# First chunk's C product as seven block products, last features of a strip in one GELU, some skips and seventh products added by transfers

## The chip, the cores and the metric

The kernel runs on one core of a Trainium2 chip. A core has a matrix engine (TensorE, PE in the profile), a vector engine (VectorE, DVE), an activation engine (ScalarE, ACT), a general engine (GpSimd, POOL) and a queue engine (SyncE, SP), which run side by side, each through its own instructions in the order of the program, and wait for each other by semaphores. Sixteen DMA engines move data. The metric is the device time of one execution in microseconds (us); less is better.

## The reference

The input x has 2048 tokens of D = 640 features, all in bfloat16. A diagonal linear recurrence with 640 complex states and a two-layer GELU network run on the same x; a gate per token mixes them:

```python
g = _sigmoid((x * gate_w).sum(-1, keepdims=True))
# recurrence: h = Lam_bar * h + B_bar @ x_t, for every token t in order
a = 2.0 * einsum("blp,dp->bld", hseq, Cmat).real + x * Dskip
# network, F = 1728
b = gelu(x @ w1 + b1) @ w2 + b2
return g * a + (1 - g) * b
```

## The kernel before

The tokens are cut into 4 chunks of 512 (`CH`). Each chunk c goes through four stages, each of which keeps TensorE streaming:

- `ff1(c)`: x @ w1 for the chunk, 13 tiles of 5 matmuls of 128x512 (L307) and a last tile of 20 small ones (L331), with a GELU on ScalarE (L316) that writes `gel`. The last features of a strip are a tile of 128 rows of which 96 go to `gel` and 32 to a helper tile `eL`, in two activations, and `load_e` brings the 32 to their place by a transfer. The gate's number for each token comes out beside it (`gz`), from which `gates(c)` (L647) makes the columns of factors `gcol`, on GpSimd, on VectorE for the last chunk.
- `ssm(c)`: B @ x, 50 matmuls (L481), evicted by ScalarE into `bu` (L484), and then the recurrence on VectorE: the state is turned by cosines and sines (`cos_in`, `sin_in`, `sum_in`, L556), scanned by two scan instructions (L573) and turned back (`cos_out`, `sin_out`, `sum_out`), into `hs[c]`. Five such groups a chunk. Four small ScalarE operations (L592) turn the end of each scan into the start of the next chunk's (`carry`).
- `fin_b(c)`: the product with w2, as a 2x2 block product with seven instead of eight block products (98 matmuls of 128x320, L738). Sums of blocks of `gel` are needed for that: a negation on ScalarE (`minus`, L687) and accumulating transfers on GpSimd's queue (`plus`, L682), together in `minus_c` and `minus_d`; for chunk 0 in `first_sums` on VectorE. The results go into tiles `gb`, scaled by half of one minus the gate (L758). `fork` copies a bank of PSUM into another with ScalarE (L750), so that two outputs can share a product. Product 7 goes into `gq` and is added to both halves of the output by an accumulating transfer (`twice`).
- the product of the states with C, and the final mix. For chunks 1 to 3 `fin_s(c)` (L900) does it with seven block products of 10 matmuls of 128x320 (L914): 70 in all, 65 for chunk 3. Its sums of blocks of `hs[c]` are M7, M6, M3 and g21 (`sum_7`, `sum_6`, `h_sums`), those of C are U7 and U6 (`sums_76`, VectorE, L875) and U5 and U4. Product 7 is added to `gb` by VectorE (`part_7`, L941), and the skip x * Dskip, times the gate, by `skip_in` (L890). Where `GS` has a tile for it (chunks 2 and 3), the scaled skip of the chunk's second half is written by ScalarE (`gated`) and added whole. `done` (L929) scales a finished bank by the gate, adds `gb` and writes `ot`, which goes out by a transfer.
- For chunk 0 `fin_a` (L806) does it plainly: 80 matmuls (L819) of 128x320 on eight banks into which ScalarE has copied the skip before (`seed`, L670, L674), and eight evictions on VectorE (L824).

In TensorE's order the stages are: ff1(0) and ssm(0) woven, ff1(1), ssm(1), fin_b(0), ff1(2), fin_a(0), ssm(2), fin_b(1), fin_s(1), ssm(3), ff1(3), fin_b(2), fin_s(2), fin_b(3), fin_s(3).

The order of each engine's instructions is fixed by the program text and by a small planner in it. `ck.pe`, `ck.act` and `ck.dve` are the planner's clocks. An operation of VectorE goes into a list with a due time and a cost (`later`); `let_out` emits those that are due, and `dve_now` emits one at once after those due before it. `scan_ops` weaves the operations of one group of the recurrence into those of the group before it. `let_out(0, c)`, the first line of `sum_7`, emits all of chunk c's recurrence that is still in the list. The rest is written by hand: a dictionary such as `{2: lambda: sum_7(1)}` calls steps in a stage's hook of that number (in `ff1` before a tile, in `ssm` before a group, in `fin_b` and `fin_s` after a product). The last lines (L1010 to L1062) are this plan.

PSUM has eight banks that are handed out in turn (`bank`); a matmul that starts a bank waits until its last reader is done. GpSimd's transfers run through one queue in order, SyncE's and ScalarE's through others.

Of the kernel before, what the change touches and what calls it, by code (L numbers as in the profile page):

```python
# [32 lines left out]
FA = 6  # L33
# [9 lines left out]
def kernel(  # L43
# [69 lines left out]
    eL = const.tile([P, CH], BF16, name="eL")  # L113
# [197 lines left out]
    def ff1_act(p, c, kf):  # L311
        s = kf if kf < FA else kf + 1 if kf < 2 * FA else FA
        for p0, p1 in ((0, RE), (RE, P)) if s == FA else ((0, P),):
            dst = eL[p0:p1, :] if p0 else gel[c][p0:p1, :, s, :]
            src = p[p0:p1, :] if p0 else p[p0:p1, :].rearrange("p (i t) -> p i t", i=2)
            nc.scalar.activation(out=dst, in_=src, func=ACT.Gelu_apprx_tanh, bias=b1_c[p0:p1, kf:kf + 1])  # L316
            act(0.69)
# [26 lines left out]
    def load_e(c):  # L344
        nc.sync.dma_start(out=gel[c][F_LAST:RE, :, KF - 1, :], in_=eL[RE:P, :].rearrange("p (i t) -> p i t", i=2))
# [17 lines left out]
    def gel_tile(c):  # L363
        gel[c] = gelp.tile([P, 2, KF, HT], BF16, name="gel")
        nc.gpsimd.memset(gel[c][RE:P, :, KH - 1, :], 1.0)
# [42 lines left out]
    part(1, 1)  # L408
    part(0, 3)
# [4 lines left out]
    turn_first(2, pA, pT)  # L414
# [232 lines left out]
    def gates(c):  # L647
# [3 lines left out]
        def f():  # L651
            for i, (m, b) in enumerate(((0.5, 0.5), (-0.5, 0.5), (0.5, -0.5), (-0.5, -0.5))[:4 if c > 0 else 3]):
# [8 lines left out]
    HALVES = ((0, HD), (HD, D))  # L661
    seeded = {}

    def cuts(ti):
        return ((0, HD), (HD, 512), (512, D)) if ti == NT - 1 else HALVES

    def skip(ti):
        dve_now(ck.pe, 0.4, lambda: nc.vector.tensor_tensor(out=xn[ti][:], in0=xn[ti][:], in1=Dbc[:], op=ALU.mult))

    def seed(ti):  # L670
        seeded[ti] = []
        for d0, d1 in cuts(ti):
            p = bank()
            nc.scalar.activation(out=p[:, 0:d1 - d0], in_=xn[ti][:, d0:d1], func=ACT.Identity)  # L674
            act(0.45)
            seeded[ti].append(p)
        if ti % TPC < TPC - 2:
            skip(ti + 2)
        if ti + TPC < NT - H:
            load_xn(ti + TPC)  # L680
# [43 lines left out]
    def twice(dst, src):  # L724
        plus(dst.rearrange("p (h d) -> p h d", h=2), src[:].rearrange("p (o d) -> p o d", o=1).to_broadcast([P, 2, HD]))

    def fin_b(c, at={}, gs=None):
# [54 lines left out]
        if c == NCH - 1:  # L782
            part_7()
            for j in range(H):
                twice(gs[j], gq[j])
# [5 lines left out]
        if c == NCH - 2:  # L791
            for j in range(H):
                twice(gs[j], gq[j])
# [5 lines left out]
        for j in range(0 if gs else H):  # L799
            twice(gbs[c * TPC + H + j][:], gq[j])  # L800
# [4 lines left out]

    def fin_a(c, at={}):  # L806
        let_out(0, c)
        for a in range(TPC):
            ti = c * TPC + a
            ot = fwork.tile([P, D], BF16, name="ot", bufs=4)  # L810
            if a < TPC - 2:
                seed(ti + 2)
            if a in at:
                at[a]()
            for i, (d0, d1) in enumerate(cuts(ti)):
                p = seeded[ti][i]
                for j in range(2 * KS):
                    CT = CT_re if j < KS else CT_im
                    nc.tensor.matmul(p[:, 0:d1 - d0], lhsT=hs[c][:, a // H, j // KS, j % KS, (a % H) * P:][:, 0:P], rhs=CT[:, j % KS, d0:d1],  # L819
                                     start=False, stop=(j == 2 * KS - 1), skip_group_check=True)  # L820
                    pe(d1 - d0)

                def f():
                    nc.vector.scalar_tensor_tensor(out=ot[:, d0:d1], in0=p[:, 0:d1 - d0], scalar=gcol[:, 0, ti:ti + 1],  # L824
                                                   in1=gbs[ti][:, d0:d1], op0=ALU.mult, op1=ALU.add)

                dve_now(ck.pe + 0.2, 0.45, f)
# [265 lines left out]
```

## Time and profile before

| what | us |
|---|---|
| median of three runs | 205.31 (205.02 to 208.02) |
| the profiled run | 205.97 |
| its span in the profile | 204.2 |
| TensorE busy | 199.4 |
| VectorE busy | 187.9 |
| ScalarE busy | 141.9 |
| GpSimd busy | 77.7 |

The span reaches from the first to the last instruction of the profile; 1.77 us of the run's time lie outside it. Of the chain that ended last, the page gives these shares by line:

```profile
PE 95%; DMA 2%; DVE 1%; SPq 0%; issue 0%; DVEq 0%
PE bank L307 27%; PE bank L738 26%; PE bank L481 21%; PE bank L914 14%; PE bank L819 5%; DMA xn<-in_A_x_dram 2%; PE bank L331 1%; DVE ot L929 0%; SPq L143 0%; PE bank L269 0%; DVEq L1088 0%; DVE colA L411 0%; PE bank L410 0%; PE bank L421 0%
```

A pair such as "PE bank L738" is an engine, the tile it wrote and the line. In a timeline a row is: start, length, engine, line, operation, output<-inputs, shape, count, and in brackets how long the engine had been idle before it and what it had waited for. A length includes the part in which the next instruction has already begun; where costs are summed, the distance of starts is meant.

### The profile page before, as it was taken

The numbers are of one execution on the slowest core, as the hardware profiler recorded it, in microseconds if no ns is written. First come the engines' busy times: TensorE is split into PE (matmuls) and PEld (weight loads), VectorE is DVE, ScalarE is ACT, GpSimd is POOL, SyncE is SP. The second block draws the span as 40 slices with busy tenths as digits, with TensorE's granted clock in tenths as the row PEclk, the third lists the DMA queues.
The fourth block names the chain that finished last, engine by engine and source line by source line (L and its number), as shares of the span: only waits on it lengthen the run. The fifth ranks groups of instructions, "written<-read, shape, count | busy, mean of one in ns | idle before, by whom it ended". The sixth has DMA issues, their size and how long they took to land.

```text
span 204.2 us, 3625 instructions
## 1 busy us (share of the span) xinstructions
PE 199.4 (98%) x1291; PEld 118.7 (58%) x1291; DVE 187.9 (92%) x292; ACT 141.9 (70%) x273; POOL 77.7 (38%) x119
## 2 busy tenths in 40 slices
PE   8899999999999999999999999999999999999994
PEld 5744544444467644676446777544446777777763
DVE  2589999999999999999999999999999999999574
ACT  3498766987867898993667674297786899245620
POOL 8385399952331299032031360032150370114000
PEclk9999999999999999999999999999999999999999
DMA  7999999999699092229878998149997699819403
GB/s 185 201 142 240 201 276 164 206 231 278 113 137 239 13 166 75 64 52 205 237 131 186 235 191 130 64 104 221 289 230 148 113 204 195 176 36 207 64 0 128
DMA packets 46374, 33.06 MB, mean 162 GB/s; under 512 B 27026, under 2 KB 42804, under 8 KB 46356
## 3 DMA queue, kind: packets, MB, share of 16 engines
q0 software_dynamic: 7040, 15.05, 42.4%
q1 hardware_dynamic: 38740, 17.29, 35.4%
q10 hardware_dynamic: 576, 0.49, 0.8%
q8 instruction: 10, 0.16, 0.3%
q14 instruction: 8, 0.07, 0.1%
HBM read 7.79 MB, written 2.62 MB: 51 GB/s over the span
## 4 chain that ended last, share of the span: by engine, by line
PE 95%; DMA 2%; DVE 1%; SPq 0%; issue 0%; DVEq 0%
PE bank L307 27%; PE bank L738 26%; PE bank L481 21%; PE bank L914 14%; PE bank L819 5%; DMA xn<-in_A_x_dram 2%; PE bank L331 1%; DVE ot L929 0%; SPq L143 0%; PE bank L269 0%; DVEq L1088 0%; DVE colA L411 0%; PE bank L410 0%; PE bank L421 0%
## 5 line engine op out<-in xcount | busy, mean ns | idle before, releaser
L316 ACT ACTIVATE gel<-bank,colB 128x512 bf16<-128x512 f32 (+1 forms) x52 | 33.6, 688 | 8.2 <-PE bank L307 7.9
L573 DVE TENSOR_TENSOR_SCAN g<-r_c,carry,v 128x512 bf16<-128x512 f32 x30 | 38.5, 1284 | 0.0
L738 PEld LDWEIGHTS <-gel 128*128 128x128 bf16 x280 | 27.3, 98 | 11.1 <-issue 0.2
L484 ACT ACTIVATE bu<-bank 128x512 bf16<-128x512 f32 x40 | 22.8, 601 | 15.4 <-PE bank L481 15.3
L738 PE MATMUL bank<-w_sb,gel 128*128 128x320 bf16 x168 | 24.3, 299 | 0.0
L758 ACT ACTIVATE gb<-bank,gcol 128x320 f32<-128x320 f32 x32 | 16.1, 527 | 7.9 <-PE bank L738 7.9
L307 PEld LDWEIGHTS <-w1a_sb 128*128 128x128 bf16 x162 | 14.0, 99 | 12.0
L307 PE MATMUL bank<-xB,w1a_sb 128*128 128x512 bf16 x90 | 19.9, 380 | 0.0
L481 PE MATMUL bank<-xB,BT_re 128*128 128x512 bf16 x75 | 18.6, 380 | 0.0
L481 PE MATMUL bank<-xB,BT_im 128*128 128x512 bf16 x75 | 18.6, 379 | 0.0
L481 PEld LDWEIGHTS <-BT_im 128*128 128x128 bf16 x100 | 9.8, 98 | 11.8
L481 PEld LDWEIGHTS <-BT_re 128*128 128x128 bf16 x100 | 9.6, 98 | 11.0
L914 PEld LDWEIGHTS <-hs 128*128 128x128 bf16 x125 | 12.0, 98 | 4.5
L929 DVE SCALAR_TENSOR_TENSOR ot<-bank,gcol,gb 128x320 bf16<-128x320 f32 (+2 forms) x25 | 12.5, 535 | 1.9 <-PE bank L914 1.2
L556 DVE TENSOR_TENSOR v<-wa,bu 128x1024 bf16<-128x1024 bf16 x20 | 13.8, 688 | 0.1
L556 DVE TENSOR_TENSOR wb<-TCOS,g 128x1024 bf16<-128x1024 bf16 x20 | 13.8, 689 | 0.0
L556 DVE TENSOR_TENSOR hs<-wb,bu 128x1024 bf16<-128x1024 bf16 x20 | 13.7, 687 | 0.0
L556 DVE TENSOR_TENSOR bu<-TSIN,g 128x1024 bf16<-128x1024 bf16 x20 | 13.8, 688 | 0.0
L556 DVE TENSOR_TENSOR wa<-TCOS,bu 128x1024 bf16<-128x1024 bf16 x20 | 13.4, 672 | 0.3 <-ACT bu L484 0.3
L556 DVE TENSOR_TENSOR bu<-TSIN,bu 128x1024 bf16<-128x1024 bf16 x20 | 13.5, 676 | 0.1
L307 PE MATMUL bank<-xB,w1b_sb 128*128 128x512 bf16 x60 | 13.4, 380 | 0.0
L738 PEld LDWEIGHTS <-N 128*128 128x128 bf16 x112 | 11.0, 98 | 4.3
(201 smaller groups left out, 401.6 us busy)
## 6 DMA issues: line engine op xcount, KB each, us to landing
out_dram<-ot SPq DMA_DIRECT2D x15, 160.0 KB, 2.4
w_sb<-in_B_w_dram SPq DMA_DIRECT2D x4, 480.0 KB, 5.8
gel<-N POOLq DMA_DIRECT2D x4, 448.0 KB, 4.9
N<-gel POOLq DMA_DIRECT2D x3, 448.0 KB, 5.1
gel<-gel POOLq DMA_DIRECT2D x3, 448.0 KB, 7.6
N<-N POOLq DMA_DIRECT2D x3, 448.0 KB, 7.5
gb<-gq POOLq DMA_DIRECT2D x4, 320.0 KB, 6.7
xn<-in_A_x_dram SPq DMA_DIRECT2D x8, 160.0 KB, 5.9
```

Of the source, the lines that this page charges most:

```text
L307: nc.tensor.matmul(p[:, t0:t1], lhsT=w, rhs=xT[c][:, kd, t0:t1], start=(kd == 0) if first is None else first, stop=(kd == last), skip_grou ...
L316: nc.scalar.activation(out=dst, in_=src, func=ACT.Gelu_apprx_tanh, bias=b1_c[p0:p1, kf:kf + 1])
L331: nc.tensor.matmul(p[:, a * NL:(a + 1) * NL], lhsT=xT[c][:, kd, a * P:(a + 1) * P], rhs=w1c[kd][:, n1c - NL:n1c], start=False, stop=(kd == ...
L481: nc.tensor.matmul(p[:], lhsT=BT[ks >= KSA][:, kd, (ks % KSA if ks < KSA else ks - KSA) * P:][:, 0:P], rhs=xT[c][:, kd, :], start=(kd == 0 ...
L484: nc.scalar.activation(out=bu[:, ri, :], in_=p[:], func=ACT.Identity)
L556: nc.vector.tensor_tensor(out=o, in0=a, in1=b, op=op)
L573: nc.vector.tensor_tensor_scan(s["g"][:, ri, :], r_c[:, ks:ks + 1].to_broadcast([P, CH]), s["v"][:, ri, :], init, ALU.mult, ALU.add)
L738: nc.tensor.matmul(p[:, 0:HD], lhsT=lhs[:, s, j * P:(j + 1) * P], rhs=rhs[:, s, :], start=fresh and s == 0, stop=s == KH - 1, skip_group_c ...
L758: nc.scalar.activation(out=gbs[ti][:, h * HD:(h + 1) * HD], in_=quad[j][name][:, 0:HD], func=ACT.Identity, scale=gcol[:, 1, ti:ti + 1])
L819: nc.tensor.matmul(p[:, 0:d1 - d0], lhsT=hs[c][:, a // H, j // KS, j % KS, (a % H) * P:][:, 0:P], rhs=CT[:, j % KS, d0:d1], start=False, s ...
L914: nc.tensor.matmul(t[j][:, d0:d1], lhsT=A[i][:, k, j * P:(j + 1) * P], rhs=B[i][:, k, d0:d1], start=fresh and k == 0, stop=k == KS - 1, sk ...
L929: dve_now(ck.pe + 0.2, 0.47, lambda: nc.vector.scalar_tensor_tensor(out=ots[ti][:, o + d0:o + d1], in0=t[j][:, d0:d1], scalar=gcol[:, 0, t ...
```

## The change

Chunk 0's C product goes through `fin_s(0)`; `fin_a`, `seed`, `cuts`, `seeds` and `sums` are removed. For that, M7 of chunk 0 is formed by a negation in the last hook of `fin_b(0)` and `sum_7(0, False)` behind it; `sums_76` moves from behind `fin_a(0)` to behind `fin_b(0)`; U5 is made by VectorE, U4 by a copy (SyncE) and an accumulation; `sum_6(0)` stands in `ff1(2)`; M3 takes M7's place in `fin_s(0)`'s hook 1. `skip_in` adds the skip for all four tiles on VectorE. Product 7 of chunks 0 and 2 is scaled by ScalarE and added by two transfers (`by_dma`) instead of by `part_7`.

The 128 rows of a strip's last features are written by one GELU into `gel`, from where `load_e` takes the 32; `ones_row(c)` then overwrites them with ones, which `gel_tile` did before at the start. It has its own place in the plan for each chunk. `gates(0)` moves to `ff1(1)` and makes four columns instead of three, `gates(1)` to `ff1(2)`, `gates(2)` from before `ssm(2)` to behind it. `first_sums` moves from tile 9 to tile 12 of `ff1(1)`.

`minus_c(1)` and `minus_d(1)` move from `fin_a(0)` into `ssm(2)`, `sum_7(1)` there from group 2 to group 3. For chunks 2 and 3 `skip_by_dma` scales half of a skip on ScalarE and adds it by a transfer, in the place of one half of `skip_in`. `minus_c(3)` moves one hook down. In the head, `turn_first(2)` stands before the `prmA` matmul.

```diff
--- before.py
+++ after.py
...
@@ -310,11 +309,9 @@
 
     def ff1_act(p, c, kf):
         s = kf if kf < FA else kf + 1 if kf < 2 * FA else FA
-        for p0, p1 in ((0, RE), (RE, P)) if s == FA else ((0, P),):
-            dst = eL[p0:p1, :] if p0 else gel[c][p0:p1, :, s, :]
-            src = p[p0:p1, :] if p0 else p[p0:p1, :].rearrange("p (i t) -> p i t", i=2)
-            nc.scalar.activation(out=dst, in_=src, func=ACT.Gelu_apprx_tanh, bias=b1_c[p0:p1, kf:kf + 1])
-            act(0.69)
+        nc.scalar.activation(out=gel[c][:, :, s, :], in_=p[:].rearrange("p (i t) -> p i t", i=2),
+                             func=ACT.Gelu_apprx_tanh, bias=b1_c[:, kf:kf + 1])
+        act(0.69)
 
     NL = F_LAST + 1
 
@@ -342,7 +339,10 @@
             load_e(c)
 
     def load_e(c):
-        nc.sync.dma_start(out=gel[c][F_LAST:RE, :, KF - 1, :], in_=eL[RE:P, :].rearrange("p (i t) -> p i t", i=2))
+        nc.sync.dma_start(out=gel[c][F_LAST:RE, :, KF - 1, :], in_=gel[c][RE:P, :, FA, :])
+
+    def ones_row(c):
+        nc.gpsimd.memset(gel[c][RE:P, :, FA, :], 1.0)
 
     def ff1(c, k0=0, at={}):
         for kf in range(k0, KF - 1):
...
@@ -649,7 +648,7 @@
         engine = nc.vector if c == NCH - 1 else nc.gpsimd
 
         def f():
-            for i, (m, b) in enumerate(((0.5, 0.5), (-0.5, 0.5), (0.5, -0.5), (-0.5, -0.5))[:4 if c > 0 else 3]):
+            for i, (m, b) in enumerate(((0.5, 0.5), (-0.5, 0.5), (0.5, -0.5), (-0.5, -0.5))):
                 engine.tensor_scalar(out=gcol[:, i, sl], in0=gz[:, sl], scalar1=m, scalar2=b, op0=ALU.mult, op1=ALU.add)
 
         if c == NCH - 1:
@@ -658,26 +657,8 @@
             f()
 
...
     def plus(dst, src):
         nc.gpsimd.dma_start(out=dst, in_=src, accum_op=ALU.add)
...
     def U54(c):
-        return (block(N3), block(gel[1][:, 0, 0:KH, :])) if c == 1 else (block(BT_re[1]), block(BT_im[1]))
+        return (block(N3), block(N2)) if c == 0 else (block(N3), block(gel[1][:, 0, 0:KH, :])) if c == 1 else (block(BT_re[1]), block(BT_im[1]))
 
     def M3(c):
+        if c == 0:
+            return M7[:]
         return narrow((N2 if c == 1 else xB)[:], KS * HT).rearrange("p (k t) -> p k t", k=KS)
 
     def add(out, x, y, op):
@@ -858,10 +811,11 @@
         return [lambda fn=add(out, x, y, op): dve_now(0, 0.8, fn) for out, x, y, op in
                 ((M7[:], a, g21, ALU.subtract), (g21, g21, d, ALU.add), (M6[:], a, g21, ALU.subtract), (M3(c), b, M6[:], ALU.add))]
 
-    def sum_7(c):
+    def sum_7(c, negate=True):
         let_out(0, c)
         (a, _), (g21, d) = state(c)
-        minus(M7[:], g21, 1.25)
+        if negate:
+            minus(M7[:], g21, 1.25)
         plus(flat(M7[:]), flat(a))
         plus(flat(g21), flat(d))
 
@@ -886,6 +840,15 @@
             ti = c * TPC + H + j
             nc.scalar.activation(out=GS[c][j], in_=xn[ti][:], func=ACT.Identity, scale=gcol[:, 0, ti:ti + 1])
             act(0.82)
+
+    GH = [t[0][:].rearrange("p k t -> p (k t)")[:, j * 2 * HD:(j + 1) * 2 * HD].bitcast(F32) for t in (BT_re, BT_im) for j in range(2)]
+
+    def skip_by_dma(c):
+        for a in range(H):
+            ti, g = c * TPC + a, GH[(c - 2) * H + a]
+            nc.scalar.activation(out=g, in_=xn[ti][:, 0:HD], func=ACT.Identity, scale=gcol[:, 0, ti:ti + 1])
+            act(0.42)
+            plus(gbs[ti][:, 0:HD], g)
 
     def skip_in(c, tiles, d0, d1, ready=0):
         for a in tiles:
@@ -899,7 +862,8 @@
 
     def fin_s(c, at={}):
         lhs, rhs = sides(c)
-        spare = [narrow(gel[1][:, 1, 0:KH, :], 4 * HD)[:, j * 2 * HD:(j + 1) * 2 * HD].bitcast(F32) for j in range(H)]
+        spare = [narrow(gel[c][:, 1, 0:KH, :], 4 * HD)[:, j * 2 * HD:(j + 1) * 2 * HD].bitcast(F32) for j in range(H)]
+        by_dma = c in (0, 2)
         A = dict(zip((1, 7, 6, 2, 5, 3, 4), lhs))
         B = dict(zip((1, 7, 6, 2, 5, 3, 4), rhs))
         X, Y, Z, Q, q = ([None] * H for _ in range(5))
@@ -920,13 +884,13 @@
             nc.scalar.activation(out=dst[j][:, d0:d1], in_=X[j][:, d0:d1], func=ACT.Identity)
             act(0.45)
 
-        def done(t, j, half, h, d0=0, d1=HD):
+        def done(t, j, half, h, d0=0, d1=HD, lag=0.2):
             ti = c * TPC + half * H + j
             first = ti not in ots
             if first:
                 ots[ti] = fwork.tile([P, D], BF16, name="ot", bufs=4)
             o = h * HD
-            dve_now(ck.pe + 0.2, 0.47, lambda: nc.vector.scalar_tensor_tensor(
+            dve_now(ck.pe + lag, 0.47, lambda: nc.vector.scalar_tensor_tensor(
                 out=ots[ti][:, o + d0:o + d1], in0=t[j][:, d0:d1], scalar=gcol[:, 0, ti:ti + 1],
                 in1=gbs[ti][:, o + d0:o + d1], op0=ALU.mult, op1=ALU.add))
             to = lambda queue, e0, e1: queue.dma_start(out=out2d[ti * P:(ti + 1) * P, e0:e1], in_=ots[ti][:, e0:e1])
@@ -947,15 +911,24 @@
             if i in at:
                 at[i]()
 
-        for j in range(H):
-            product(X, 1, j, True)
-            fork(j, Y)
+        def first():
+            for j in range(H):
+                product(X, 1, j, True)
+                fork(j, Y)
+
+        def seventh():
+            for j in range(H):
+                product(Q, 7, j, True)
+                q[j] = spare[j] if c in (1, 2) else fwork.tile([P, HD], F32, name="gq", bufs=2)[:]
+                ti = c * TPC + H + j
+                nc.scalar.activation(out=q[j], in_=Q[j][:, 0:HD], func=ACT.Identity, scale=gcol[:, 3, ti:ti + 1] if by_dma else 1.0)
+                act(0.44)
+            for j in range(H if by_dma else 0):
+                twice(GS[c][j] if c in GS else gbs[c * TPC + H + j][:], q[j])
+
+        first()
         hook(0)
-        for j in range(H):
-            product(Q, 7, j, True)
-            q[j] = spare[j] if c == 1 else fwork.tile([P, HD], F32, name="gq", bufs=2)[:]
-            nc.scalar.activation(out=q[j], in_=Q[j][:, 0:HD], func=ACT.Identity)
-            act(0.44)
+        seventh()
         hook(1)
         if c < NCH - 1:
             W = [None] * H
@@ -972,11 +945,17 @@
                 product(X, 3, j)
                 done(X, j, 0, 1)
             for j in range(H):
-                skip_in(c, (H + j,), 0, D, ck.pe)
-                part_7(j)
+                if not by_dma:
+                    skip_in(c, (H + j,), 0, D, ck.pe)
+                    part_7(j)
                 product(Z, 4, j)
-                done(Z, j, 1, 0)
-            for j in range(H):
+                if not by_dma:
+                    done(Z, j, 1, 0)
+            for j in range(H):
+                if by_dma:
+                    if c > 0:
+                        skip_in(c, (H + j,), 0, D, ck.pe + 1.4)
+                    done(Z, j, 1, 0, lag=1.6)
                 done(W, j, 1, 1)
             return
         for j in range(H):
@@ -1001,30 +980,35 @@
         skip(c * TPC + a)
         skip(c * TPC + a + 1)
 
-    ssm(0, {KSA: lambda: (factors(), gates(0))}, early)
+    ssm(0, {KSA: lambda: factors()}, early)
     gel_tile(1)
 
-    ff1(1, 0, {3: lambda: (w_minus(0), w_plus(TA, B12)),
+    ff1(1, 0, {3: lambda: (w_minus(0), w_plus(TA, B12)), 4: lambda: (gates(0), ones_row(0)),
                5: lambda: (w_minus(1), w_plus(B12, TB)),
-               9: lambda: (first_sums(), w_plus(TB, TA), w_plus(TC, TB))})
+               9: lambda: (w_plus(TB, TA), w_plus(TC, TB)),
+               12: first_sums})
     ssm(1, {2: lambda: fold(0), 4: lambda: fold(1)})
     load_xT(2)
-    fin_b(0, {1: lambda: fold(2), 2: lambda: fold(3), 3: lambda: fold(4)})
+    fin_b(0, {1: lambda: fold(2), 2: lambda: fold(3), 3: lambda: (minus(M7[:], hs[0][:, 1, 0], 1.25), fold(4))})
+    sums_76()
+    sum_7(0, False)
+    U5, U4 = U54(0)
+    dve_now(0, 0.95, lambda: nc.vector.tensor_tensor(out=U5, in0=C22, in1=U6, op=ALU.add))
     load_skip()
+    copy(U4, C21)
     gel_tile(2)
-    gates(1)
-    ff1(2, 0, {8: lambda: skips(0), 10: lambda: seed(0), 11: lambda: seed(1)})
-    fin_a(0, sums(1))
+    plus(U4, U6)
+    ones_row(1)
+    ff1(2, 0, {7: lambda: (sum_6(0), gates(1)),
+               10: lambda: (skips(0), skips(0, H)),
+               11: lambda: skip_in(0, (H, H + 1), 0, D)})
+    fin_s(0, {0: lambda: skip_in(0, (0, 1), 0, D, ck.pe - 1.0), 1: h_sums(0)[3]})
+    for a in range(TPC):
+        load_xn(TPC + a)
+    ssm(2, {0: lambda: minus_c(1), 1: lambda: minus_d(1), 3: lambda: sum_7(1), KS - 1: lambda: (skips(1), skips(1, H))})
+    load_xT(3)
     gates(2)
-    sums_76()
-    ssm(2, {2: lambda: sum_7(1), KS - 1: lambda: (skips(1), skips(1, H))})
-    load_xT(3)
+    ones_row(2)
     U5, U4 = U54(1)
     fin_b(1, {1: lambda: (sum_6(1), copy(U4, C21)),
               4: lambda: (copy(U5, C22), plus(U4, U6), plus(U5, U6)),
@@ -1051,12 +1035,12 @@
     ff1(3, 0, {1: next_54, 5: lambda: (skips(2), let_out(0, 2)), 7: load_early})
     for a in range(H):
         load_xn((NCH - 1) * TPC + a, narrow(w1b_sb[:], H * D)[:, a * D:(a + 1) * D])
-    fin_b(2, {1: lambda: (gated(2), sum_6(2), skips(3, H)),
-              2: lambda: (gates(3), minus_c(3)),
-              3: lambda: (gated(3), skip_in(2, (0, 1), 0, HD))}, GS[2])
-    fin_s(2, {0: lambda: (skip_in(2, (0, 1), HD, D, ck.act + 0.5), h_sums(2)[3]()), 1: lambda: (minus_d(3), skips(3))})
+    fin_b(2, {1: lambda: (gated(2), sum_6(2), skip_by_dma(2), skips(3, H)),
+              2: lambda: (gates(3), ones_row(3), gated(3)),
+              3: lambda: minus_c(3)}, GS[2])
+    fin_s(2, {0: lambda: (h_sums(2)[3](), skip_in(2, (0, 1), HD, D, ck.act + 0.5)), 1: lambda: (minus_d(3), skips(3))})
     fin_b(3, {0: lambda: (let_out(1e9), [f() for f in h_sums(3)]),
-              3: lambda: skip_in(3, (0, 1), 0, HD)}, GS[3])
+              1: lambda: skip_by_dma(3)}, GS[3])
     skip_in(3, (H, H + 1), 0, D)
     skip_in(3, (0, 1), HD, D)
     fin_s(3)
```

## The prediction

> **What bounds the kernel now.** I read the page's busy shares first, then the chain of waits, then the timelines of VectorE, ScalarE and GpSimd around the change. Busy shares and 40 slices:
>
> ```profile
> PE 199.4 (98%) x1291; PEld 118.7 (58%) x1291; DVE 187.9 (92%) x292; ACT 141.9 (70%) x273; POOL 77.7 (38%) x119
> ...
> DVE  2589999999999999999999999999999999999574
> ...
> PEclk9999999999999999999999999999999999999999
> ```
>
> TensorE sets the end, and VectorE is full from the fourth slice to the 37th. So work added to VectorE in the middle can't be absorbed: it delays what stands behind it. The chain of waits (start, length, what) where chunk 0's C product (L819) stands:
>
> ```profile
> 85.10 10.87 PE bank L819 x80
> 95.96 10.79 PE bank L481 x50
> 106.75 1.90 PE bank L738 x14
> 108.66 0.02 issue
> 108.68 11.57 PE bank L738 x84
> 120.25 9.56 PE bank L914 x70
> ```
>
> TensorE waits for nobody between 7.4 and 200.5 us. The two forms of the C product stand here side by side: 10.87 for 80 matmuls, 9.56 for 70. The VectorE timeline at the end of chunk 1's scan (L556 hs):
>
> ```profile
> 94.37 0.70 DVE L556 TENSOR_TENSOR hs<-wb,bu 128x1024 bf16<-128x1024 bf16 x1
> 94.97 0.56 DVE L824 SCALAR_TENSOR_TENSOR ot<-bank,gcol,gb 128x320 bf16<-128x320 f32 x1
> 96.00 0.55 DVE L824 SCALAR_TENSOR_TENSOR ot<-bank,gcol,gb 128x320 bf16<-128x320 f32 x1 [0.47 <-PE bank L819]
> 96.47 0.98 DVE L875 TENSOR_TENSOR CT_re<-CT_re,CT_im 128x1600 bf16<-128x1600 bf16 x1
> 97.48 0.99 DVE L875 TENSOR_TENSOR xA<-CT_re 128x1600 bf16<-128x1600 bf16 x1
> ```
>
> hs(1) is done at 95.06. Its first reader outside VectorE is the negation L688 that `sum_7(1)` puts on ScalarE, in that timeline:
>
> ```profile
> 100.81 1.26 ACT L688 ACTIVATE M<-hs 128x1280 bf16<-128x1280 bf16 x1
> 101.97 1.10 ACT L484 ACTIVATE bu<-bank 128x512 bf16<-128x512 f32 x2
> ...
> 107.28 0.28 ACT L592 ACTIVATE e<-g,nsL 128x1 f32<-128x1 bf16 x1
> ...
> 108.21 0.90 ACT L750 ACTIVATE bank<-bank 128x320 f32<-128x320 f32 x2
> ```
>
> It began 5.8 us after hs(1) was done. Behind it, in ScalarE's order, stand evictions, the carries, and the copies of two banks (L750) with which TensorE starts product Y of `fin_b(1)` at 108.68.
>
> **The change, part by part.**
>
> TensorE: ten matmuls of 0.136 us fewer, 9.56 for 10.87: −1.31. In the head, the transposes of `turn_first(2)` now stand ahead of the matmul behind whose copy (colA) TensorE waited 0.18 + 0.04 us: 0 to −0.27, taken at −0.1.
>
> ScalarE: eight seeds go (0.39 each, 3.1 us) and one 0.68 us GELU per chunk; skips by transfer add four activations. It idles 3.43 us before 97.08 already: worth nothing by itself.
>
> VectorE, by program order up to the last write of hs(1). Fifteen instructions stand ahead of it that stood behind or did not exist (start-to-start cost of the nearest rows):
> - four skip_in of 128x640 at 0.80: 3.2
> - two more evictions (ot) at 0.46: 0.92
> - U7 and U6 (L875, the two rows above), moved up, and the like U5: 3 × 1.0 = 3.0
> - M3(0), 128x1280, as L847: 0.74
> - of chunk 2, woven in: one scan 1.2 and four of 0.60: 3.6
>
> Together 11.46 us, so hs(1) ends at 95.06 + 11.46 = 106.5 at the earliest. No idle time ahead of 94.37 since 39 us gives any of it back.
>
> ScalarE order after the change: six evictions of `ssm(2)`, then sum_7(1)'s negation, four evictions, carries, the forks. `ssm(2)` starts 1.4 us sooner, so the sixth eviction is over by about 102 and ScalarE waits for hs(1). From 106.5: negation 1.16, four evictions 4 × 0.50, carries 0.93 (107.28 to 108.21), first fork 0.42, handing over 0.1 = 4.6. Product Y starts at 111.1. It started at 108.68, and would start at 107.3 if only the TensorE savings counted. So TensorE waits 3.8 us there, and all behind it is 2.4 later than before. The eight banks do not stop TensorE sooner: four hold unread sums of `ssm(2)`, two product X. Nor is any of the delay recovered later, as TensorE is full to the end.
>
> VectorE's own new waits ahead of hs(1), which no row of before shows, add to this:
> - M3(0) waits for M6(0), a chain: hs accumulated by transfer (landed about 80 to 81, the median of such a transfer being 5.6), ScalarE's negation to 82.3, then in GpSimd's queue an issue that waits for the copy of U4 (its like, BT_im<-CT_im, 8.3 us; N<-CT_im 4.6) and for another transfer and a memset, and 4.8 us to land: 86.5 to 88.7. VectorE comes there at about 87 to 88. From 0 to 1.5 us.
> - The loads of x and of Dbc queue behind the new accumulations of M7 and hs (this pair took 3.6 us at 103.6 to 107.2), landing at 81 to 84, where VectorE wants them at 82 to 83: 0 to 1.0.
>
> Lower ends of zero, as nothing becomes ready sooner; I take 0.8 for both together: under the middle of 0 to 2.5, as the first landing lies at the need and the two waits can't add up in full (VectorE that came late by the second finds M6(0) landed).
>
> Later parts. `gates(2)` and a memset now stand in GpSimd's queue ahead of the accumulation b += N2 that `fin_b(1)`'s last product reads. The same four instructions took:
>
> ```profile
> 75.84 6.13 POOL L653 TENSOR_SCALAR gcol<-gz 128x4 f32<-128x4 f32 x4
> ...
> 95.41 0.95 POOL L653 TENSOR_SCALAR gcol<-gz 128x4 f32<-128x4 f32 x4
> ```
>
> By the longer row 1.3 us of TensorE's time, by the shorter none. Beside the longer one VectorE ran scans and products of two tiles without a break; beside the shorter it idled 0.47 us and evicted banks. The new place is of the first kind, but less of the 1.3 is sure than that: I take 0.5, from 0 to 1.3. The Trainium skill (GPSIMD Engine Reference, 1. Specifications) says that GpSimd shares its SBUF interfaces with VectorE, with contention when VectorE's instructions are in a 2-port mode or have two SBUF inputs. Both rows agree with it, and by it the sum would be 0.8 us higher.
>
> hs(2), needed by `fin_b(2)`'s forks through the like negation, ends around 154, which banks of `ff1(3)` cover: 0. hs(3) and M3(3) end at 191.8 and 195.3 for needs of 194.6 and over 198: 0. For chunk 3, the two half skips given to transfers (two activations, two accumulations) lie in GpSimd's queue ahead of w1c_lo<-gq. That one already kept VectorE 0.79 us, with 1.7 us of slack to TensorE's last banks against about 2 us added: 0.2 at the end. Chunk 2's transfers in the place of two seventh products and two half skips spare VectorE 2 × 0.88 + 2 × 0.46 = 2.7 us, where it feeds no one who waits: 0. The moved first_sums, ones_row(0) and minus_c(3) have several us to their readers: 0; without that cover, first_sums' accumulation of about 5 us would be the price.
>
> Sum: +2.4 (savings of 1.4 and the wait of 3.8 within it) + 0.8 + 0.5 + 0.2 = +3.9. On the profiled run of 205.97 (span 204.2, and 1.77 outside it) that is 209.9; that run lies 0.66 above the median of 205.31, so for the median 209.2.
>
> **Rivals.** What a measurement can tell from no change is about 2%, here 4.1 us: 201.2 to 209.4.
>
> No wait (faster). If hs(1) ends by 102.5, four evictions and the rest still let product Y start by 107.1, and 1.4 to 1.6 are gained: 203.8. That needs 4 of the 11.46 us of VectorE to vanish. For it: the weaving could be undone where VectorE runs ahead. Against: its queue is in order. 0.12.
>
> The wait at its floor. All transfers of chunk 0 in time: +2.4 and little else, 207.7 or less. The needs and landings above cross within 1 us, so this is near. 0.26.
>
> Late transfers (slower). U4's copy takes 8.3 us or more, M6(0) lands at 92 instead of 88: TensorE waits some 3 us before product 6 of `fin_s(0)`, VectorE as long, and hs(1) slips by 4 to 5: 213. It decides from M6 landing after about 89. Most copies of this kind took 4 to 5 us. 0.08.
>
> Slow clock after the wait (slower). TensorE stands still for 3.8 to 4.6 us with no row of before to compare: there it never waited over 0.8 us, and PEclk is 9 in every slice. When it first set out, nine matmuls of 128x512 (L266) took 2.72 us, where 65 later took 14.03, so nine 1.94: 0.8 us was lost in starting, and lost again it gives 210.0. The Trainium skill (TensorE: Matmul & The Clock Gate, Why this matters for your kernels) asks for no TensorE gap over about 3 us, since one idle window brings the clock down to half; by that rule, with the 3.4 us of matmuls that it takes to recover, an estimate of the loss is 1.7 us and the time 210.9. Whether the gap holds a whole window is open. 0.10.
>
> **How the numbers follow.** Forecast (wait plus some late input) 0.42, split by the bound at 209.4 as 0.20 and 0.22; with the floor 0.26 and no wait 0.12, within 2% is 0.58. Late transfers, slow clock and the other part are 0.40. Faster by over 2% would take 4.1 us, where TensorE saves 1.6 at most: 0.02, for what I mistake. The range reaches from 206.4, below the floor by the 1.3 of the savings, to 212.0, the forecast with the long `gates` row and 1.5 more of late input. It leaves out no wait and late transfers, some 0.2.
>
> **What would show it.** Before product Y of `fin_b(1)`, TensorE idle for 3 to 5 us, released by ScalarE; there ScalarE idle before the 128x1280 negation, released by VectorE's hs. VectorE idle by about 1 us near M3(0) and the products with Dbc. L914 with 275 + 70 matmuls, and no 128x320 seeds. If ScalarE finds hs(1) ready, or TensorE runs through, I am wrong; if TensorE waits in `fin_s(0)`, the late transfers have it; and a PEclk under 9 after the gap is the slow clock.

## The result and the profile after

The changed kernel took 221.14 us (median of four runs, 217.72 to 224.26) against 205.3; the ratio is 1.0612, with a 95% interval of 1.0446 to 1.0777. Taken again beside its first experiments it came out at 220.46 against 205.96, ratio 1.0652 (1.0559 to 1.0744). It is slower by far more than 209.2, and above the range. The ratios count undisturbed runs alone and the medians all runs, and since the first profile (223.0) fell into a disturbed run, the lines below are from that of the second set (221.35, span 219.6), the same kernel.

Busy shares and slices of the changed kernel:

```profile
PE 204.0 (93%) x1281; PEld 120.0 (55%) x1281; DVE 189.7 (86%) x292; ACT 141.6 (64%) x275; POOL 86.9 (40%) x132
...
PE   8999999999999999499947999999999898999982
...
DVE  1699999999999988399999686799999999699393
...
PEclk9999999999999999889995899999999999999998
```

TensorE has ten matmuls fewer and is busy longer, 204.0 for 199.4, and PEclk has two dents: matmuls ran at a lower clock. VectorE, which was full from the fourth slice to the 37th before, now has holes in which it waits. TensorE's timeline, the rows from 70 us on that stand behind a wait of over 0.5 us (the bracket: how long, and for whom):

```profile
92.37 2.83 PE L878 MATMUL bank<-xA,M 128*128 128x320 bf16 x10 [3.07 <-DMA M<-hs]
...
116.39 3.89 PE L719 MATMUL bank<-w_sb,gel 128*128 128x320 bf16 x14 [4.32 <-ACT bank L731]
...
174.25 2.06 PE L719 MATMUL bank<-TA,gel 128*128 128x320 bf16 x14 [0.63 <-ACT bank L731]
...
183.65 1.52 PE L878 MATMUL bank<-CT_im,hs 128*128 128x320 bf16 x10 [0.81 <-ACT bank L884]
...
197.25 2.08 PE L719 MATMUL bank<-TB,N 128*128 128x320 bf16 x14 [0.51 <-DMA N<-N]
...
212.79 1.52 PE L878 MATMUL bank<-CT_im,xB 128*128 128x320 bf16 x10 [0.98 <-DVE ot L893]
```

Three places. At 92, product 6 of `fin_s(0)` waits for the transfer into M6(0). At 116, product Y of `fin_b(1)` waits for ScalarE's forks. From 174 on there are five small waits in chunks 2 and 3, four of them shown and one of 0.22. The second is the forecast one, and its cause stands where it was expected, in ScalarE's timeline (column in brackets as above):

```profile
111.89 1.27 ACT L669 ACTIVATE M<-hs 128x1280 bf16<-128x1280 bf16 x1 [5.27 <-DVE hs L555]
113.06 2.04 ACT L483 ACTIVATE bu<-bank 128x512 bf16<-128x512 f32 x4
...
115.90 0.76 ACT L731 ACTIVATE bank<-bank 128x320 f32<-128x320 f32 x2
```

The negation that was 5.8 us behind hs(1) now waits 5.27 us for it, with four evictions, the carries and the forks behind it. What hs(1) itself waited for is in VectorE's timeline:

```profile
83.20 1.78 DVE L661 TENSOR_TENSOR xn<-xn,Dbc 128x640 bf16<-128x640 bf16 x4 [1.53 <-DMA Dbc<-in_A_Dskip_dram]
...
92.45 0.82 DVE L800 TENSOR_TENSOR M<-hs,M 128x1280 bf16<-128x1280 bf16 x1 [3.68 <-DMA M<-hs]
...
111.17 0.68 DVE L555 TENSOR_TENSOR hs<-wb,bu 128x1024 bf16<-128x1024 bf16 x1
```

The last line is hs(1)'s last write. And what M6(0) waited for is in GpSimd's timeline, and in the row of the DMA issues from 72 to 97 us (KB, us to landing) for U4's copy:

```profile
85.74 0.89 POOL L664 DMA_DIRECT2D N<-xA  x1 [9.20 <-PE bank L878]
86.30 0.86 POOL L345 MEMSET gel<- 32x512 bf16 x1
86.77 1.22 POOL L664 DMA_DIRECT2D M<-hs  x1
```

```profile
N<-CT_im SPq DMA_DIRECT2D x1, 400.0 KB, 9.6
```

The copy was issued at 75.55 and landed 9.6 us later, at 85.1. Only then could the accumulation on top of it (N<-xA) be issued, and M6(0)'s, ready since ScalarE's negation, stood behind that in the queue. The profile names TensorE for the 9.20 us of waiting, but in six other profiles with this copy (the first one, e1, e2, e5, e7, e8) the accumulation also comes some 0.6 us after the copy's landing, whichever engine is named there; so the copy is taken as what it waited for.

So the time can be read stage by stage, by the starts of the same rows in the timelines and chains (before, after): start of `ssm(2)` 95.80, 99.22; product Y of `fin_b(1)` 108.68, 116.39; `fin_s(1)` 120.25, 130.87; end of TensorE 200.5, 215.0; span 204.2, 219.6. The loss grows by 3.4 (the wait for M6(0) and its lower clock, less what ten matmuls save), 4.3 (the forks), 2.9 (the clock), 3.9 (chunks 2 and 3) and 0.9 (the end): 15.4 together. The first two, 7.7 at product Y, are by VectorE's path the forecast 2.4 and VectorE's own waits ahead of hs(1), 1.53 and 3.68: the negation, not TensorE's own wait at 92, sets when product Y starts.

### The profile page after: what moved, and what is told of

The parts are those of the page before. It is cut to its first block, busy times and chain, and to the rows that moved or that the text cites. A ratio compares the mean times of both kernels' runs of the same rounds, so it can differ in the third digit from the quotient of the medians.

```text
span 221.2 us, 3628 instructions
## 1 busy us (share of the span) xinstructions
PE 202.9 (92%) x1270; PEld 119.0 (54%) x1281; DVE 189.7 (86%) x292; ACT 142.1 (64%) x275; POOL 89.8 (41%) x132
## 4 chain that ended last, share of the span: by engine, by line
PE 37%; DMA 22%; DVE 11%; POOL 8%; issue 8%; ACT 6%; SPq 6%; DVEq 0%; POOLq 0%; ACTq 0%
PE bank L719 13%; PE bank L306 12%; PE bank L878 6%; DMA TC<-TB 5%; PE bank L480 5%; DMA N<-N 4%; DVE g L572 4%; DMA w1c_lo<-gq 3%; DMA w_sb<-TB 3%; SPq L167 3%; DMA M<-hs 2%; DVE ot L893 2%; DMA gel<-gelN 2%; DMA w1c_hi<-in_B_w_dram 2%; POOL e L580 1%
## 5 line engine op out<-in xcount | busy, mean ns | idle before, releaser
L719 PEld LDWEIGHTS <-gel 128*128 128x128 bf16 x280 | 28.4, 102 | 23.5 <-issue 10.9
L312 ACT ACTIVATE gel<-bank,colB 128x512 bf16<-128x512 f32 x52 | 33.0, 694 | 5.2 <-PE bank L306 5.0
L483 ACT ACTIVATE bu<-bank 128x512 bf16<-128x512 f32 x40 | 22.1, 599 | 16.7 <-PE bank L480 11.8
L719 PE MATMUL bank<-w_sb,gel 128*128 128x320 bf16 x168 | 26.4, 314 | 5.6 <-ACT bank L731 5.6
L893 DVE SCALAR_TENSOR_TENSOR ot<-bank,gcol,gb 128x320 bf16<-128x320 f32 (+2 forms) x33 | 16.5, 535 | 6.4 <-PE bank L878 5.4
L878 PEld LDWEIGHTS <-hs 128*128 128x128 bf16 x165 | 15.8, 98 | 7.3 <-issue 1.4
L719 PEld LDWEIGHTS <-N 128*128 128x128 bf16 x112 | 11.4, 102 | 5.8 <-DMA N<-N 0.8
L884 ACT ACTIVATE bank<-bank 128x320 f32<-128x320 f32 (+2 forms) x23 | 9.2, 412 | 8.2 <-PE bank L878 8.2
```

The lines of the kernel that those rows point to most:

```text
L312: nc.scalar.activation(out=gel[c][:, :, s, :], in_=p[:].rearrange("p (i t) -> p i t", i=2), func=ACT.Gelu_apprx_tanh, bias=b1_c[:, kf:kf + 1])
L483: nc.scalar.activation(out=bu[:, ri, :], in_=p[:], func=ACT.Identity)
L719: nc.tensor.matmul(p[:, 0:HD], lhsT=lhs[:, s, j * P:(j + 1) * P], rhs=rhs[:, s, :], start=fresh and s == 0, stop=s == KH - 1, skip_group_c ...
L878: nc.tensor.matmul(t[j][:, d0:d1], lhsT=A[i][:, k, j * P:(j + 1) * P], rhs=B[i][:, k, d0:d1], start=fresh and k == 0, stop=k == KS - 1, sk ...
L884: nc.scalar.activation(out=dst[j][:, d0:d1], in_=X[j][:, d0:d1], func=ACT.Identity)
L893: dve_now(ck.pe + lag, 0.47, lambda: nc.vector.scalar_tensor_tensor(out=ots[ti][:, o + d0:o + d1], in0=t[j][:, d0:d1], scalar=gcol[:, 0, t ...
```

## The experiments

Each ran beside the kernel before on the same chip. Ratios are to it. e5, e7, e8 and e9 ran on another chip than the rest, so a gain between the two groups is better read from the ratios. The intervals of e1, e2, e5 and e8 overlap with that of `again`: there the rows of the traces carry the reading, not the time.

| run | what | median us | ratio (95%) |
|---|---|---|---|
| again | the changed kernel | 220.46 | 1.0652 (1.0559 to 1.0744) |
| e1_sum7_late | sum_7(1) behind product Y | 217.93 | 1.0533 (1.0445 to 1.0620) |
| e2_no_xT | without the load of x for chunk 2 | 218.16 | 1.0574 (1.0516 to 1.0631) |
| e4_fin_a | chunk 0 by fin_a | 208.92 | 1.0126 (1.0077 to 1.0175) |
| e5_no_part5 | chunks 2 and 3 as before | 220.79 | 1.0670 (1.0592 to 1.0748) |
| e7_m6_first | M6(0) ahead of U4 | 216.44 | 1.0490 (1.0428 to 1.0551) |
| e8_warm | matmuls in the wait | 219.33 | 1.0623 (1.0562 to 1.0683) |
| e9_fin_a_no5 | e4 and e5 together | 207.26 | 1.0048 (1.0014 to 1.0082) |
| e3_head | before, with the head's order | 205.59 | 0.9979 (0.9958 to 1.0000) |
| e10_m6_no_skip0 | e7 without chunk 0's skip | 212.93 | 1.0348 (1.0305 to 1.0392) |
| e11_m6_sum7 | e7 and e1 together | 213.49 | 1.0397 (1.0347 to 1.0446) |
| e12_best | e9, minus_c(3) behind gated(3) | 208.17 | 1.0058 (1.0021 to 1.0094) |

**Again.** No edit.

> The changed kernel as it is. If the wait for TC<-TB (3.7 us in the first trace) and the wait before product Y of fin_b(1) (5.6) belong to the change, both stand in this trace too, within 1 us. If the first is a matter of chance between two transfers, it differs by more than 1 us here, and the time of the runs spreads with it (217.7 to 224.3 so far).

The wait before product Y was there both times (5.61 and 4.32, a little further apart than expected). That for TC<-TB was not: in the first profile TensorE waited 2.34 and 1.34 us for it in `fin_b(0)`, here only 0.37, for gel<-N. No other profile shows more than 0.28 for it (e7), and the main loss does not rest on it. In the first profile the wait for M6(0) was only 0.65, since TensorE had already lost 3.7 before it.

**Chunk 0's product by fin_a.** The rest stays as changed, save that `minus_c(1)`, `minus_d(1)`, `sum_7(1)` and `gates(1)` go back to about where they stood.

```diff
-    fin_b(0, {1: ..., 2: ..., 3: lambda: (minus(M7[:], hs[0][:, 1, 0], 1.25), fold(4))})
+    fin_b(0, {1: ..., 2: ..., 3: lambda: fold(4)})
...
-    fin_s(0, {0: lambda: skip_in(0, (0, 1), 0, D, ck.pe - 1.0), 1: h_sums(0)[3]})
+    fin_a(0, {0: lambda: minus_c(1), 1: lambda: minus_d(1)})
+    sums_76()
```

> All of the change but chunk 0's seven products: chunk 0 goes through fin_a with seeds as before; the rest as changed. Theory of the queue: no wait before fin_b(1)'s product Y, and what remains is the collision and chunk 2's and 3's transfers: 206 to 212. If the seven products of chunk 0 were not the main loss: 214 or more.

208.92: TensorE ran through from 0.77 to 162 us at full clock. So some five percent (1.0652 less 1.0126) are chunk 0's seven products with what they need, and 1.3% the rest as it stands beside `fin_a`.

**M6(0) ahead of U4 in GpSimd's queue.**

```diff
-    plus(U4, U6)
-    ones_row(1)
-    ff1(2, 0, {7: lambda: (sum_6(0), gates(1)),
+    ff1(2, 0, {7: lambda: (sum_6(0), plus(U4, U6), ones_row(1), gates(1)),
```

> The accumulation into U4 and ones_row(1) move behind the accumulation into M6(0) in GpSimd's queue. Theory of the late transfer (M6(0) was queued behind U4's accumulation, which waited 9.5 us for U4's copy): M6(0) is issued at 84 to 85 instead of 87 to 89, TensorE's wait for M<-hs falls from 3.1 to under 1, VectorE's from 3.7 to under 1.5; the wait before product Y stays at 4 to 6, as hs(1) and TensorE come sooner by about the same; time lower by 2 to 3.5. Rival, that M6(0) is late because hs lands late: M<-hs still waited for by 2 us or more.

M6(0) was issued at 81.60, sooner than expected, and nobody waited for it. From VectorE's timeline and TensorE's:

```profile
106.97 0.69 DVE L555 TENSOR_TENSOR hs<-wb,bu 128x1024 bf16<-128x1024 bf16 x1
```

```profile
112.19 3.89 PE L719 MATMUL bank<-w_sb,gel 128*128 128x320 bf16 x14 [4.44 <-ACT bank L731]
```

hs(1) ended at 107.66 with 1.01 us of VectorE's own waits ahead of it instead of 5.21, and product Y started 4.2 us sooner, by just that difference. The wait before it stayed: both sides of it had moved together. The ratio fell by 0.016, 3.3 us, and its interval lies below that of `again`. The late transfer is shown as a cause, and the queue ahead of M6(0) as its place.

**The skip of chunk 0 left out, on top of that.**

```diff
-               10: lambda: (skips(0), skips(0, H)),
-               11: lambda: skip_in(0, (H, H + 1), 0, D)})
-    fin_s(0, {0: lambda: skip_in(0, (0, 1), 0, D, ck.pe - 1.0), 1: h_sums(0)[3]})
+               10: lambda: (skips(0), skips(0, H))})
+    fin_s(0, {1: h_sums(0)[3]})
```

> As e7_m6_first, with the skip of chunk 0 left out (its four skip_in of 128x640 on VectorE, 3.2 us). Theory of the queue: hs(1) ends 3.2 us sooner (104.5 instead of 107.7), the wait before product Y falls from 4.4 to 1.2, the clock does not fall, so 3.2 + 2.2 = 5.4 less, save 1.3 to 1.7 for the accumulation into b behind gates(2), which then is waited for: 211 to 213 after 216.4. Rival, that hs(1) is held by transfers: wait still over 3, time lower by under 2.

212.93, within the forecast, but not quite by its reasons. ScalarE's timeline shows why the wait is gone altogether:

```profile
102.27 1.27 ACT L669 ACTIVATE M<-hs 128x1280 bf16<-128x1280 bf16 x1
103.43 2.22 ACT L483 ACTIVATE bu<-bank 128x512 bf16<-128x512 f32 x4
106.07 0.42 ACT L731 ACTIVATE bank<-bank 128x320 f32<-128x320 f32 x1 [0.41 <-PE bank L719]
```

The negation finds hs(1) ready, and the fork now waits for TensorE. hs(1) ended at 101.67, which fits the prediction's point of about 102.5 (e7, at 107.66, lies beyond it). That is 6.0 sooner than in e7 and not 3.2: VectorE stood 1.0 ahead at 78 us already, and one scan and three products fewer of chunk 2 are woven in ahead. So the run takes off more than the skip. The wait for b behind `gates(2)`, for which 1.3 to 1.7 were taken off, did not come, as `gates(2)` took 1.29 us here. But 2.8 us more of waits for ScalarE stand in chunks 1 and 2 (0.5 in `fin_b(1)`, 3.3 in `fin_s(2)`, of which 1.0 stood there in e7), so taking away 4.4 of waiting and some 2 of slow clock (84 matmuls had taken 13.76 in e7) brought 3.5, or 2.9 by the ratios. That these amounts nearly cancel is luck.

**sum_7(1) behind product Y.**

```diff
-    ssm(2, {0: lambda: minus_c(1), 1: lambda: minus_d(1), 3: lambda: sum_7(1), KS - 1: ...})
+    ssm(2, {0: lambda: minus_c(1), 1: lambda: minus_d(1), KS - 1: ...})
...
-    fin_b(1, {1: lambda: (sum_6(1), copy(U4, C21)),
+    fin_b(1, {1: lambda: (sum_7(1), copy(U4, C21)),
+              2: lambda: sum_6(1),
```

> sum_7(1) moves from group 3 of ssm(2) behind product Y of fin_b(1), and sum_6(1) two hooks down. Theory of the queue (the negation that waits for hs(1) holds the evictions and forks behind it on ScalarE): the wait of 5.6 us before product Y is gone and TensorE's clock stays full there (2.9 us more); M6(1) comes 1 to 3 us late in fin_s(1); time lower by 5 to 8. Rival, that fin_b(1) waits for something else at that place (b, N2, or banks): lower by under 2.

The wait before product Y is gone, so ScalarE's order is its cause. The gain, 2.5 us, is half of what was expected, for three rows that stand behind it in TensorE's timeline:

```profile
118.55 2.06 PE L719 MATMUL bank<-TA,gel 128*128 128x320 bf16 x14 [0.77 <-ACT bank L731]
127.44 1.52 PE L878 MATMUL bank<-CT_re,M 128*128 128x320 bf16 x10 [1.67 <-ACT gb L739]
129.93 1.52 PE L878 MATMUL bank<-CT_im,hs 128*128 128x320 bf16 x10 [0.97 <-ACT bank L884]
```

The negation still waits for hs(1), and what now stands behind it is `fin_b(1)`'s later evictions. Together with e7:

> Both moves together, M6(0) ahead of U4 and sum_7(1) behind product Y. If they add: 216.4 less 2.5 to 4, that is 212.5 to 214. If the late sums of chunk 1 take it back in fin_s(1): 215 to 217.

They add (213.49), and it is still 4% slower than before.

**Matmuls in the wait.** Their results are read by nobody; the wait itself is not touched.

```diff
         both("X", a, W(0, 0), True)
+        if c == 1:
+            for j in range(H):
+                quad[j]["Y"] = bank()
+                for _ in range(9):
+                    nc.tensor.matmul(quad[j]["Y"][:], lhsT=ident[:], rhs=TCOS[:, 0, :], start=True, stop=True)
         fork("X", "Y")
```

> Eighteen matmuls of 128x512 whose results nobody reads stand between products X and Y of fin_b(1): TensorE works in the time in which it waited (4.3 to 5.6 us; they take 3.9). Theory of the clock (after a wait of that length the matmuls run at half speed for some 5 us, 2.9 us lost): product Y starts at the same time and the 84 matmuls from it on take 11.6 instead of 14.4 us; time lower by 2 to 3. Rival, that these 14.4 us come from VectorE's and ScalarE's lateness in fin_b(1) and not from the clock: same time, still over 13.5.

First the changed kernel's TensorE row by stretches (us, busy, weight loads, VectorE, ScalarE, GpSimd, then the granted clock, DMA share and GB/s), then TensorE's timeline of the one with the added matmuls:

```profile
116.00:118.00 2.00, 1.61 (x7) 0.91 (x7) 2.00 (x4) 0.66 (x3) 1.94 (x4) 0.50 0.98 232
118.00:120.00 2.00, 2.00 (x9) 1.15 (x8) 2.00 (x4) 0.53 (x1) 0.07 (x1) 0.50 1.06 199
120.00:122.00 2.00, 2.00 (x10) 1.11 (x8) 2.00 (x3) 1.59 (x2) 0.89 (x1) 0.50 0.04 9
122.00:124.00 2.00, 2.00 (x15) 1.40 (x14) 2.00 (x5) 0.20 (x1) 1.50 (x2) 0.91 1.06 199
```

```profile
109.18 4.05 PE L762 MATMUL bank<-TCOS,ident 128*128 128x512 bf16 x17
114.95 2.06 PE L719 MATMUL bank<-w_sb,gel 128*128 128x320 bf16 x14 [1.72 <-ACT bank L732]
...
126.28 2.08 PE L719 MATMUL bank<-w_sb,gel 128*128 128x320 bf16 x14 [1.66 <-DMA gel<-N]
```

In the changed kernel the clock granted after the wait was 0.50 for some six us, and 84 matmuls took 14.48 us instead of 11.57. With the wait filled, 14 matmuls take 2.06 at once, not 3.89, and PEclk has no dent in any slice. That is the clock, shown. But from product Y to the start of `fin_s(1)` only 1.1 us are left of the 2.9 (13.24 instead of 14.32 by the starts of the rows), and the time, 219.33 for 220.46, can't be told from no change, where 2 to 3 less was expected: TensorE then waits 1.66 us for b (gel<-N), whose accumulation was issued behind `gates(2)`:

```profile
113.12 6.04 POOL L652 TENSOR_SCALAR gcol<-gz 128x4 f32<-128x4 f32 x4
119.23 0.52 POOL L345 MEMSET gel<- 32x512 bf16 x1
119.81 0.89 POOL L664 DMA_DIRECT2D gel<-N  x1
```

In the changed kernel TensorE does not wait there: `gates(2)` took 6.04 us in its first profile and 2.93 in its second, and after the slow matmuls TensorE comes later to b.

**Without the load of x for chunk 2.**

```diff
     ssm(1, {2: lambda: fold(0), 4: lambda: fold(1)})
-    load_xT(2)
```

> The transposing load of x for chunk 2 is left out, so chunk 2 is computed from chunk 1's x. Theory of the collision (the accumulation TC<-TB and this load share the DMA engines from 57 to 67 us and slow each other): TC<-TB lands 5 to 6 us after its issue instead of 11, TensorE waits 0 to 0.5 for it instead of 3.7, the clock stays at 1.0 there, time lower by 4 to 6. Rival, that the chain of w2's sums is late because gates(0) and ones_row(0) stand in GpSimd's queue ahead of it: TensorE still waits 2 us or more.

Its profile shows no wait for TC<-TB at all, but then `again` has none either: the gain of about 1.6 us (0.008 of the ratio) goes with a wait for M6(0) of 2.09 in the place of 3.07, which other profiles of the same code up to there have as well (1.58 to 2.72 in e1, e5 and e8). Without the load TC<-TB's two transfers landed in 3.6 and 3.2 us, with it in 5.1 and 4.7 in `again` and 11.4 and 10.8 in the first profile. The run can't tell what brought about the long ones; that stays open.

**Chunks 2 and 3 as before.**

```diff
-        by_dma = c in (0, 2)
+        by_dma = c == 0
...
-    fin_b(2, {1: lambda: (gated(2), sum_6(2), skip_by_dma(2), skips(3, H)),
-              2: lambda: (gates(3), ones_row(3), gated(3)),
-              3: lambda: minus_c(3)}, GS[2])
+    fin_b(2, {1: lambda: (gated(2), sum_6(2), skips(3, H)),
+              2: lambda: (gates(3), ones_row(3), minus_c(3)),
+              3: lambda: (gated(3), skip_in(2, (0, 1), 0, HD))}, GS[2])
...
-              1: lambda: skip_by_dma(3)}, GS[3])
+              3: lambda: skip_in(3, (0, 1), 0, HD)}, GS[3])
```

> The changed kernel with chunks 2 and 3 as before (product 7 by part_7 for chunk 2, half skips by skip_in on VectorE, minus_c(3) one hook up). Theory of the added transfers (negations and accumulations queued behind the added activations and transfers make the forks of fin_b(2), the product with N of fin_b(3) and the last gb late, 0.6 + 0.8 + 0.2 + 0.5 + 1.0 us of TensorE and 1.5 at the end): lower by 2.5 to 4. Rival, that these waits come from chunk 0's part further up and only shift: lower by under 1.

A miss: nothing gained. The waits of 0.63 and 0.51 are gone, and the rival, that they would only shift, has the size right but not the place: one of 2.03 for an ot of VectorE stands in `fin_s(3)`, and the last 20 matmuls of the chain take 4.30 us; 20 of the same shape took 2.88 in e9. VectorE works without a break in the last 7 us before that ot, so with chunk 0's work still on it the time that these transfers take off it is needed at the end. Both undone:

> The changed kernel with chunk 0 through fin_a and chunks 2 and 3 as before: what is left are one GELU per strip, ones_row, the moved gates and first_sums, and turn_first(2) in the head. If the loss lies in chunk 0's seven products and chunk 2's and 3's transfers alone: 203.5 to 205.5, a little under before, as TensorE's waits in the head (0.7 for xn and 0.3 for colA) are gone. If the moved gates and ones_row cost something: 206 or more.

207.26, ratio 1.0048, against 1.0126 with the transfers: here they cost 1.6 us, and beside chunk 0's seven products nothing that shows. So their price seems to depend on whether VectorE is late. The 207.26 are still above the expected 205.5: TensorE's one wait (1.04, for a fork in `fin_s(2)`) comes from ScalarE, which waited 1.82 us for ones_row(3)'s memset before minus_c(3)'s negation.

```diff
-              2: lambda: (gates(3), ones_row(3), minus_c(3)),
-              3: lambda: (gated(3), skip_in(2, (0, 1), 0, HD))}, GS[2])
+              2: lambda: (gates(3), ones_row(3), gated(3)),
+              3: lambda: (minus_c(3), skip_in(2, (0, 1), 0, HD))}, GS[2])
```

> As e9_fin_a_no5, but gated(3) stands before and minus_c(3) behind the hook in which ones_row(3) is issued, so that ScalarE does not wait for that memset (1.8 us there, then 1.04 on TensorE). If that was its only loss: TensorE runs through, 0.65 ahead of before, 204.6 to 205.6 in the undisturbed runs. If something else holds TensorE in fin_s(2): 206 to 207 as e9.

A miss too: that wait fell to 0.57, but 0.66 for gel<-N and 0.27 for BT_im stand earlier, and the time is that of e9, as its rival said (206.81 in the profiled run).

**The head alone, in the kernel before.**

```diff
     part(1, 1)
+    turn_first(2, pA, pT)
     part(0, 3)
```

> The kernel before, with turn_first(2) ahead of the prmA matmul, nothing else. If the 0.65 us that TensorE gains in the head reach the end: 204.6 to 205.0 against 205.3 to 206.0. If VectorE, which is full from 39 us on, sets the end in fact: no change. If an earlier ssm(1) is what lets the load of x for chunk 2 meet TC<-TB, some runs come out 4 to 6 us longer.

All of TensorE's waits behind 0.77 us are gone, that of 0.7 for xn included, and the median is 205.59 for 205.82: 0.2%, at the edge of what five rounds tell. No other version tried comes out under the kernel before.

## Why the prediction was wrong

The wait that was forecast came, and its path was right. What failed is the size of the late input of chunk 0, taken at 0.8, and the step "where it feeds no one who waits: 0" for chunk 2's transfers; and the slow clock was left out of the sum. In the trace product Y started 7.7 later where 2.4 + 0.8 were said, the clock then cost 2.9, and from `fin_s(1)` to the end 4.8 came where 0.2 was said.

- The ledger of VectorE was right, and all fifteen instructions of it stand in the timeline of e7. It put hs(1)'s end at 106.5 at the earliest; with M6(0) in time it was 107.66, of which 1.01 are waits.
- So was the path from there: negation, four evictions, carries, fork, 4.6 us. In `again` it took from 111.89 to product Y at 116.39, 4.5. The wait of 3.8 to 4.6 was 4.32, in e7 4.44.
- The late input of chunk 0 was the term that was mis-sized. Taken at 0.8 with 2.5 as its end, it was 1.53 + 3.68 on VectorE. M6(0) was to land at 88.7 at the latest and landed at 92.3. Of the 3.6 us, 1.3 are the copy of U4, bounded by 4.6 and 8.3, which took 9.6; 1.6 are the accumulation into U4 and the memset, which stood between its landing and M6(0)'s issue and for which that latest time had nothing; and 0.8 is M6(0)'s own landing, 5.56 instead of 4.8. The copy alone is not it: in e8 it took 8.2, and M6(0) was still waited for, 3.58 by VectorE and 1.91 by TensorE. That the copy was long because the loads of x and Dbc and two accumulations were on the queues beside it is likely and not shown. The rival "late transfers", given 0.08, is what happened, with the mechanism as described.
- The slow clock, given 0.10, happened too, twice: behind the wait for M6(0) (ten matmuls in 2.83 for 1.52) and behind that for the forks. By the start of the trace it was priced at 0.8; the second alone cost 2.9. The sentence on the Trainium skill beside it (TensorE: Matmul & The Clock Gate, Why this matters for your kernels), which asks for no TensorE gap over about 3 us, agrees with 4.32 of waiting and then a clock of 0.50; but waits of 2.03 and 2.09 (e5, e2) were followed by a clock of 0.50 too, so here shorter gaps cost it as well. The 1.7 worked out from it was too little, as the low clock lasted about six us.
- The long form of `gates(2)`, 6.04 us, came in the first profile, e5, e7 and e8; in `again` it was 2.93. It was taken at 0.5 between 0 and 1.3; with the clock kept up (e8) it was worth 1.66, and in the changed kernel nothing. Beside the 6.04 of e8 VectorE ran scans and products of two tiles without a break; in e10 it happened to idle 1.51 us there, and the four instructions took 1.29. The Trainium skill's rule of shared interfaces (GPSIMD Engine Reference, 1. Specifications) agrees with these rows; what decides between 2.93 and 6.04 beside a full VectorE no run here shows.
- Chunks 2 and 3 were put at 0 and 0.2 and were 3.9 in the trace. The step that failed is "where it feeds no one who waits: 0": it looked at VectorE, which the transfers relieve, and not at the queues that they are put on. Two activations more stand ahead of `fin_b(2)`'s forks (0.63), and N<-N landed 9.5 us after its issue, behind the accumulations of product 7 (9.5 in e4 too, 4.4 before and 4.6 in e9, which have no such accumulations there), with chunk 3's gel<-N, gb, xB and w1c_lo queued after it on GpSimd:

```profile
184.65 2.44 POOL L664 DMA_DIRECT2D w1a_sb<-gel  x2
187.74 0.90 POOL L664 DMA_DIRECT2D N<-N  x1 [0.65 <-PE bank L878]
197.83 0.86 POOL L664 DMA_DIRECT2D gel<-N  x1 [9.20 <-DMA N<-N]
...
200.75 2.45 POOL L664 DMA_DIRECT2D w1c_lo<-gq  x1
```

- Head: 0.1 was said, 0.27 at most. The start of `ssm(0)` moved by 0.4 (`again`) to 1.3 us (e7), as the wait for xn went as well, and in e3, where it moved by 1.0, 0.2 to 0.4 us of the time are left of it.
- And the rivals were weighed as if one excluded the other. They feed each other here: a late transfer delays VectorE, so the negation, so TensorE, and the wait that results is long enough to cost the clock. Most of them came together.

## What to carry to other kernels

Where one engine is saturated, count what a change puts ahead of the value that other engines need next, in its order; here that gave hs(1)'s time to 0.2 us, while 1.3 us of saved matmuls were never in play. A transfer moved off a full engine is not free: price its place in its queue, by the slowest landing of its kind and not the median, with the instructions that stand between that landing and the issue, and ask what is queued behind it. When a wait over some 2 us on TensorE is part of a forecast, add the slow clock after it to the same case.

## What the runs showed that was not expected

- The wait from which the clock falls is no sharp length: behind 1.58 and 1.91 us (e5, e8) ten matmuls of 128x320 took 1.53, behind 2.03 (e5, near the end) 2.34, behind 2.09 (e2) 2.46, behind 2.72 (e1) 1.76 and the next ten 2.87, behind 3.07 (`again`) 2.83.
- In the first profile, while the load of x for chunk 2 and the accumulation TC<-TB ran side by side, TC<-TB took 11 us to land, against 5 before, and the load 14.8 against 9.8. But before and in `again` the two ran side by side as well, so that alone does not explain it; one profile shows it, and its cause is open.
